# Local attention products with V: two heads in one matmul, or one head per matmul in four tiles

## The chip, the core and the metric

The kernel runs on one core of one Trainium2 chip. The metric is the device time of one execution in microseconds (us). PE is the matrix engine (TensorE), PEld its weight loads, DVE, ACT, POOL and SP are the vector, scalar, GpSimd and sync engines.

## What is computed

Attention over 8 batches, 8 heads, 576 positions and 64 values per head, in float32. In heads 0 to 3 a query sees itself and the 31 positions before it ("local"); in heads 4 to 7 it sees the earlier positions that are equal to its own modulo 32 ("strided"). The result, 4608 tokens of 512 values, goes through a mixture of 8 experts: every token takes the expert with the largest gate logit, its output is scaled by that gate probability.

```python
attn = softmax(where(mask, scale * q @ k.T, -1e9))      # mask local for h < 4, else strided
x = (attn @ v).transpose(0, 2, 1, 3).reshape(4608, 512)
expert_idx = argmax(x @ w_gate, axis=1)
for e in range(8):
    xe = x[expert_idx == e]
    out[expert_idx == e] = gate_w * (relu(xe @ w1[e]) @ w2[e])
```

## The kernel before, in words

**Attention (kind "A" in the planner).** Each batch has two local head pairs (`hp` 0 and 1), two strided ones, and five score banks of 128x512. A bank goes through: scores on PE (L713, L719 local, L728 strided), maximum and subtraction on DVE (L768, L773), exp on ACT (L777), sum and reciprocal on DVE (L781 to L784), normalization on POOL (L788), four transposes on PE (L793), and a copy to the tile `pT` (L295 or L297, in `evac`).

**Products with V.** `local(hp)` in `av_ops` multiplies the probabilities of 16 query blocks of 32 with V. Line 849 takes both heads of the pair in one matmul: the weights are 64 keys by 128 values (two heads of 64), the moving side 64 columns (two heads by 32 queries). Half of each 128x64 result is one head's V with the other head's probabilities and is never read. A float32 matmul shows in the trace as two passes, so a unit (one batch, one head pair) has 32 matmul records and 32 weight loads, and there are 16 units. Two tiles work side by side: `y` 0 on partitions 0 to 63, `y` 1 on 64 to 127. Four copies of 64x256 (`e_ev`, two `y` by two heads) bring the halves that count to `xT`. `strided(hp)` does the same with the helper `av_mm` (L816), which takes one head per matmul at tile position (64y, 64h), so four tiles; with `hp` 0 it also holds the last 64 local queries of both pairs, with 64 weight columns and 32 moving columns. Nothing of `strided` changes.

**Experts.** `window` handles 256 or 512 tokens of one expert, `slot` 128. A weight chunk of 1 MB (`raw`) is loaded by SP, rounded by ACT (`whi`, L384), its remainder taken by DVE (`wlo`, L388), and PE does three matmuls for every product (L507 to L509, L480 to L482; L579 to L581 and L607 to L609 in slots). Four windows (kind "F") are planned while attention still runs, once the tokens of the first four batches are routed; all other work (kind "B") after attention.

**The order of the work** is written out by a planner before the kernel is built. `add(engine, cost, emit, deps, get=, put=, prio=, ins=)` enters a piece of work with an estimated cost in ns; `Line.pick` takes the piece that can start first, by priority among those close together, and `issue` emits it. So each engine's order of instructions is fixed by these estimates; the chip keeps only the data dependences.

**Instructions.** `Line.fetch` models that PE's instructions come in blocks of 256 over DMA. `ins` counts a piece's PE instructions (a pass and its weight load are two). When a piece crosses into the next block, its cost grows by what is missing until `next_block`; then the next block is set to arrive 3500 ns later, plus the backlog that the planner sees on the DMA queues (`self.bus - began`), up to a cap. `PIECES` is 4, so the cap is 625 ns.

```python
if n and self.count >= 256:
    self.count -= 256
    at = t + cost * left / n
    still = max(0.0, self.next_block - at)
    began = at + still
    self.next_block = began + 3500.0 + min(max(0.0, self.bus - began), 2500.0 / PIECES)
```

Of the kernel before, what the change touches and what calls it, by code (L numbers as in the profile page):

```python
# [23 lines left out]
QB = 32  # L24
# [20 lines left out]
PIECES = 4  # L45
# [19 lines left out]
PE, ACT, DVE, POOL, SP = "PE", "ACT", "DVE", "POOL", "SP"  # L65
EITHER = (ACT, DVE)
# [21 lines left out]
class Line:  # L88
# [20 lines left out]
    def add(self, *a, **k):  # L109
        op = Op(*a, **k)  # L110
        self.pending[op.kind] += 1
        for d in op.deps:
            if d.done is None:
                op.left += 1
                d.users.append(op)
            else:
                op.ready = max(op.ready, d.done + self.LAG[d.where])
        if not op.left:
            self.waiting.append(op)
        return op  # L120
# [60 lines left out]
    def fetch(self, t, n, cost):  # L181

        still = 0.0
        left = 256 - self.count
        self.count += n
        if n and self.count >= 256:
            self.count -= 256
            at = t + cost * left / n
            still = max(0.0, self.next_block - at)
            began = at + still  # L190
            self.next_block = began + 3500.0 + min(max(0.0, self.bus - began), 2500.0 / PIECES)
        return still

    def issue(self, t, e, op):
# [41 lines left out]
def act_ns(n):  # L236
    return 25 + 0.91 * n


def dve_ns(n):  # L240
    return 68 + 1.04 * n


def both(n):
    return {ACT: act_ns(n), DVE: dve_ns(n)}
# [31 lines left out]
def moe_attn(ctx, tc, lqk, vl, sqk, vs, wg, wcat, blob, out):  # L277
    nc = tc.nc
# [8 lines left out]
    def bank(slot):  # L287
        return ps.tile([128, 512], F32, name=f"b{slot.which}", bufs=1)

    def buf(pool, shape, dt, name, slot):  # L290
        return pool.tile(shape, dt, name=f"{name}{slot.which}", bufs=1)

    def evac(e, out, in_):
        if e == DVE:
            nc.vector.tensor_copy(out=out, in_=in_)  # L295
        else:
            nc.scalar.copy(out=out, in_=in_)  # L297
# [36 lines left out]
    add = line.add  # L334
# [301 lines left out]
    U = {}  # L636
# [35 lines left out]
    loads = {}  # L672
# [138 lines left out]
    def probs_of(b, pair, y, cols):  # L811
        k, n = WHERE[pair]
        return U[b, "pT", k][64 * y:64 * y + 64, 128 * n + cols.start:128 * n + cols.stop]

    def av_mm(av, c0_, w, h, y, lhsT, rhs):
        nc.tensor.matmul(av[64 * h:64 * h + 64, c0_:c0_ + w], lhsT, rhs, start=True, stop=True, tile_position=(64 * y, 64 * h))  # L816

    xslots = {}
    evs = {}

    def x_tile(g):
        if g not in xslots:
            xslots[g] = Slot("xT", 0)
        return xslots[g]

    def av_ops(b):
        g, bb = divmod(b, GB)
        off = bb * S
        xs = x_tile(g)
        evs.setdefault(g, {})[bb] = []  # L830

        def xT():
            if ("xT", g) not in U:
                U["xT", g] = buf(xtp, [128, 4, GB * S], F32, "xT", xs)
            return U["xT", g]

        def local(hp):
            st = {}

            def e_av(_):  # L840
                xT()
                vt = U[b, "vl", hp]
                st["av"] = [bank(x) for x in vsl]
                for m in range(4):
                    for i in range(2):
                        n = 2 * m + i
                        for y in range(2):
                            both_heads = probs_of(b, ("l", hp, m), y, slice(0, 128)).rearrange("p (h i q) -> p h i q", h=2, i=2)
                            nc.tensor.matmul(st["av"][y][:, 64 * n:64 * n + 64], vt[64 * y:64 * y + 64, n, :],  # L849
                                             both_heads[:, :, i, :], start=True, stop=True, tile_position=(64 * y, 0))  # L850

            vsl = [Slot("b", 2), Slot("b", 2)]
            get = list(vsl)
            if bb == 0 and hp == 0:
                get.append(xs)
            p = time_of(b, hp + 0.2)
            a = add(PE, 960, e_av, [U[b, "C", hp], loads[b, "vl", hp][0]], get=get, ins=64,
                    put=[U[b, "ps", hp], loads[b, "vl", hp][1]], prio=p)
            for y in range(2):
                for h in range(2):  # L860
                    def e_ev(e, y=y, h=h):
                        hs = slice(64 * h, 64 * h + 64)
                        dst = xT()[hs, hp, off:off + 512].rearrange("p (n y q) -> p n y q", y=2, q=QB)[:, :, y, :]
                        evac(e, dst, st["av"][y][hs, :].rearrange("p (n h q) -> p n h q", h=2, q=QB)[:, :, h, :])

                    evs[g][bb].append(add(EITHER, both(256), e_ev, [a], put=[vsl[y]], prio=p + 1))

        def strided(hp):
            st = {}
            c1 = 5 * RG  # L870

            def e_av(_):
                vst = U[b, "vs"]
                av = st["av"] = [bank(x) for x in vsl]
                for t in range(5):
                    for y in range(2):
                        for h in range(2):
                            av_mm(av[y], RG * t, RG, h, y, vst[64 * y:64 * y + RG, 5 * hp + t, 64 * h:64 * h + 64],
                                  probs_of(b, ("s", hp, t), y, slice(64 * h, 64 * h + RG))[0:RG])
                if hp == 0:  # L880
                    for i in range(2):
                        vt = U[b, "vl", i]
                        for y in range(2):
                            for h in range(2):
                                av_mm(av[y], c1 + QB * i, QB, h, y, vt[64 * y:64 * y + 64, 8, 64 * h:64 * h + 64],
                                      probs_of(b, ("lx", 0, 4), y, slice(64 * h + 32 * i, 64 * h + 32 * i + 32)))
                else:
                    for y in range(2):
                        for h in range(2):
                            av_mm(av[y], c1, LASTG, h, y, vst[64 * y:64 * y + LASTG, 10, 64 * h:64 * h + 64],  # L890
                                  probs_of(b, ("sx", 0, 5), y, slice(64 * h, 64 * h + LASTG))[0:LASTG])

            vsl = [Slot("b", 2), Slot("b", 2)]
            p = time_of(b, 3.2 + hp)
            deps = [loads[b, "vs"][0]] + ([U[b, "C", 2], U[b, "C", 3], loads[b, "vl", 0][0], loads[b, "vl", 1][0]] if hp == 0
                                          else [U[b, "C", 3], U[b, "C", 4]])
            put = [loads[b, "vs"][1]] + ([U[b, "ps", 2], U[b, "ps", 3], loads[b, "vl", 0][1], loads[b, "vl", 1][1]] if hp == 0
                                         else [U[b, "ps", 3], U[b, "ps", 4]])
            a = add(PE, 950 if hp == 0 else 770, e_av, deps, get=vsl, put=put, prio=p, ins=112 if hp == 0 else 96)
            for y in range(2):  # L900
                def e_ev(e, y=y):
                    xv = xT()[:, 2 + hp, off:off + S].rearrange("p (a r) -> p r a", r=STR)
                    dst = xv[:, 0:30, :].rearrange("p (t y l) a -> p t y l a", y=2, l=3)[:, :, y, :, :]
                    evac(e, dst, st["av"][y][:, 0:c1].rearrange("p (t l a) -> p t l a", l=3, a=SR))

                def e_ev2(e, y=y):
                    av = st["av"][y]
                    if hp == 0:
                        x0 = off + 512 + QB * y
                        evac(e, xT()[:, 0:2, x0:x0 + QB], av[:, c1:c1 + 2 * QB].rearrange("p (a q) -> p a q", q=QB))  # L910
                    else:
                        xl = xT()[:, 2 + y, off:off + S].rearrange("p (a r) -> p r a", r=STR)
                        evac(e, xl[:, 30:32, :], av[:, c1:c1 + LASTG].rearrange("p (r a) -> p r a", a=SR))

                evs[g][bb].append(add(EITHER, {ACT: 440, DVE: 620}, e_ev, [a], put=[vsl[y]], prio=p + 1))
                evs[g][bb].append(add(EITHER, both(80), e_ev2, [a], put=[vsl[y]], prio=p + 1))

        local(0)
        local(1)
        strided(0)  # L920
        strided(1)
# [306 lines left out]
    with tc.manual_schedule():  # L1228
# [9 lines left out]
        for b in range(B):  # L1238
# [5 lines left out]
            g, bb = divmod(b, GB)  # L1244
            p, f = time_of(b + 1, 2), 2000.0
            if g == EG - 1:
                p, f = (time_of(b, NBK - 0.5), 100.0) if bb else (time_of(b + 1, 0), 2000.0)
# [32 lines left out]
        start = F_START + F_SPAN * len(EXP)  # L1280
# [185 lines left out]
```

## Time and profile before

| what | value |
|---|---|
| median of 3 runs | 696.97 us (695.48 to 701.06) |
| profiled execution | 694.56 us, its span 692.4 us |
| PE matmuls busy | 645.1 us (93%), 6468 records |
| DVE / ACT / POOL busy | 408.2 / 374.8 / 167.0 us |
| local products with V (L849) on PE | 512 records, 34.4 us |

The span runs from the first to the last instruction; the execution's own time is 2.2 us longer. The trace gives start and duration of every instruction, what ended an engine's idle time ("<-"), and the chain of work that ended last. "issue" in that chain is time in which the engine waited for nothing that the profile shows.

### The profile page before, as it was taken

The page shows a single profiled execution, that of the slowest core. Times are in us where ns is not written, and L with a number is a line of the kernel's source. Part 1 is how long each engine was busy: PE and PEld are TensorE (multiplying, and loading weights), DVE is VectorE, ACT ScalarE, POOL GpSimd, SP SyncE. Part 2 cuts the span into 40 slices and gives each one's busy share as a digit, 9 for nine tenths or more (in the row PEclk, how much of TensorE's full clock was granted, in tenths as well). Part 3 has the DMA queues.
Part 4 walks back from the last instruction along what each step waited for, and adds up shares of the span by engine and source line. Part 5 has one row for each costly group of instructions (what it writes and reads, how often), then busy time and mean ns, then how long its engine had stood idle before and what let it go on. Part 6 is the DMA issues. An engine that isn't in the chain of part 4 may idle for free.

```text
span 692.4 us, 15650 instructions
## 1 busy us (share of the span) xinstructions
PE 645.1 (93%) x6468; PEld 546.1 (79%) x6472; DVE 408.2 (59%) x752; ACT 374.8 (54%) x675; POOL 167.0 (24%) x232
## 2 busy tenths in 40 slices
PE   5899798999999997799999999998999999999993
PEld 4677677789888886698888888887888888978882
DVE  5577777684756669774327565246573347664271
ACT  2566466574746663654337474256582366663471
POOL 2222534530414226412015021042030051110120
PEclk9999999599999999999999999999999999999998
DMA  9968959972675455987246867337776258582430
GB/s 300 325 196 281 311 173 385 371 251 78 218 235 194 161 183 167 382 294 239 68 136 228 279 235 270 122 127 269 244 257 235 75 203 320 202 292 74 137 122 6
DMA packets 84170, 149.60 MB, mean 216 GB/s; under 512 B 4861, under 2 KB 33533, under 8 KB 84096
## 3 DMA queue, kind: packets, MB, share of 16 engines
q1 hardware_dynamic: 75264, 124.73, 53.6%
q0 software_dynamic: 6432, 20.26, 7.8%
q10 hardware_dynamic: 2400, 3.58, 1.5%
q8 instruction: 52, 0.85, 0.5%
q14 instruction: 22, 0.18, 0.1%
HBM read 129.38 MB, written 20.22 MB: 216 GB/s over the span
## 4 chain that ended last, share of the span: by engine, by line
PE 78%; DMA 6%; DVE 5%; issue 4%; ACT 3%; POOL 2%; another core or an unknown queue 0%; POOLq 0%; SPq 0%; ACTq 0%; DVEq 0%
PE b L482 8%; PE b L480 8%; PE b L509 8%; PE b L481 8%; PE b L507 8%; PE b L508 7%; PE b L849 5%; DMA raw<-in_wcat_dram 5%; PE b L728 3%; DVE wlo L388 3%; PE b L719 3%; PE b L793 2%; PE b L456 2%; PE b L993 2%; PE b L580 2%
## 5 line engine op out<-in xcount | busy, mean ns | idle before, releaser
L388 DVE TENSOR_TENSOR wlo<-raw,whi 128x1024 fp32r<-128x1024 f32 x160 | 190.9, 1226 | 84.3 <-ACT whi L384 81.3
L384 ACT CAST whi<-raw 128x1024 fp32r<-128x1024 f32 x160 | 163.5, 1053 | 63.9 <-PE b L482 46.4
L507 PE MATMUL b<-xh,whi 128*128 128x256 f32 (+1 forms) x384 | 125.5, 327 | 0.0
L509 PE MATMUL b<-xh,wlo 128*128 128x256 f32 (+1 forms) x384 | 123.3, 321 | 1.8 <-DVE wlo L388 1.5
L508 PE MATMUL b<-xl,whi 128*128 128x256 f32 (+1 forms) x384 | 122.5, 319 | 0.3 <-DVE xl L352 0.3
L480 PE MATMUL b<-whi,hh 128*128 128x512 f32 x256 | 103.1, 403 | 3.2 <-ACT hh L517 3.1
L482 PE MATMUL b<-whi,hl 128*128 128x512 f32 x256 | 101.3, 396 | 4.1 <-DVE hl L520 4.1
L517 ACT ACTIVATE hh<-b 128x256 fp32r<-128x256 f32 (+1 forms) x96 | 43.4, 453 | 107.8 <-PE b L509 103.1
L481 PE MATMUL b<-wlo,hh 128*128 128x512 f32 x256 | 100.2, 391 | 0.0
L520 DVE SCALAR_TENSOR_TENSOR hl<-b,hh 128x256 fp32r<-128x256 f32 (+1 forms) x96 | 48.2, 506 | 73.3 <-ACT hh L517 73.2
L423 POOL DMA_INDIRECT out_dram<-y,oids x24 | 24.9, 1039 | 240.9 <-ACT y L416 237.9
L509 PEld LDWEIGHTS b<-xh,wlo 128*128 128x128 f32 x384 | 72.9, 190 | 9.2 <-DVE wlo L388 3.7
L508 PEld LDWEIGHTS b<-xl,whi 128*128 128x128 f32 x384 | 73.0, 190 | 7.5 <-DVE xl L352 0.5
L507 PEld LDWEIGHTS b<-xh,whi 128*128 128x128 f32 x384 | 72.9, 190 | 6.9
L788 POOL TENSOR_TENSOR prob<-prob,ri 128x512 f32<-128x512 f32 x40 | 43.3, 1082 | 103.8 <-DVE ri L784 79.5
L482 PEld LDWEIGHTS b<-whi,hl 128*128 128x128 f32 x256 | 48.0, 188 | 17.4 <-DVE hl L520 6.3
L297 ACT COPY xT<-b 64x256 f32<-64x256 f32 (+3 forms) x122 | 42.8, 418 | 34.8 <-PE b L849 20.7
L480 PEld LDWEIGHTS b<-whi,hh 128*128 128x128 f32 x256 | 48.3, 189 | 11.9 <-ACT hh L517 4.3
L481 PEld LDWEIGHTS b<-wlo,hh 128*128 128x128 f32 x256 | 48.4, 189 | 8.1
L352 DVE TENSOR_TENSOR xl<-b,xh 128x256 fp32r<-128x256 f32 (+1 forms) x48 | 23.4, 505 | 30.3 <-ACT xh L350 27.4
L781 DVE TENSOR_REDUCE sm<-prob 128x8 f32<-128x512 f32 x40 | 27.0, 676 | 18.8 <-ACT prob L777 18.5
L579 PE MATMUL b<-whi,sxh 128*128 128x256 f32 x128 | 37.6, 294 | 0.0
(164 smaller groups left out, 1044.0 us busy)
## 6 DMA issues: line engine op xcount, KB each, us to landing
raw<-in_wcat_dram SPq DMA_DIRECT2D x80, 1024.0 KB, 8.5
lqk_sb<-in_lqk_dram SPq DMA_DIRECT2D x16, 592.0 KB, 5.8
sqk_sb<-in_sqk_dram SPq DMA_DIRECT2D x16, 576.0 KB
vt<-in_vl_dram SPq DMA_DIRECT2D x16, 576.0 KB, 5.1
xd<-xr SPq DMA_DIRECT2D x24, 264.0 KB, 5.6
vst<-in_vs_dram SPq DMA_DIRECT2D x8, 704.0 KB, 11.3
xd<-xr ACTq DMA_DIRECT2D x12, 264.0 KB, 2.0
xg<-xd,ids POOLq DMA_INDIRECT x24
```

What stands on the lines that cost most here:

```text
L297: nc.scalar.copy(out=out, in_=in_)
L384: nc.scalar.copy(out=self.hi[:, sl], in_=self.raw[:, sl])
L388: nc.vector.tensor_tensor(out=self.lo[:, sl], in0=self.raw[:, sl], in1=self.hi[:, sl].bitcast(F32), op=ALU.subtract)
L480: nc.tensor.matmul(Y[t], H["h"][:, ts], ch.hi[:, w], start=(j == 0), stop=False)
L481: nc.tensor.matmul(Y[t], H["h"][:, ts], ch.lo[:, w], start=False, stop=False)
L482: nc.tensor.matmul(Y[t], H["l"][:, ts], ch.hi[:, w], start=False, stop=(j == 7))
L507: nc.tensor.matmul(b, ch.hi[:, w], X["h"][:, dc, :], start=(dc == 0), stop=False)
L508: nc.tensor.matmul(b, ch.hi[:, w], X["l"][:, dc, :], start=False, stop=False)
L509: nc.tensor.matmul(b, ch.lo[:, w], X["h"][:, dc, :], start=False, stop=(dc == 3))
L517: nc.scalar.activation(out=H["h"][:, 0:n], in_=H["b"][:, 0:n], func=AF.Relu)
L520: nc.vector.scalar_tensor_tensor(out=H["l"][:, 0:n], in0=H["b"][:, 0:n], scalar=0.0, in1=H["h"][:, 0:n].bitcast(F32), op0=ALU.max, op1=ALU ...
L788: nc.gpsimd.tensor_tensor(out=pv, in0=pv, in1=st["ri"].unsqueeze(2).broadcast_to([128, 8, 64]), op=ALU.mult)
```

## The change

In `local`, line 849 becomes a loop over the two heads that calls `av_mm`: 64 weight columns, 32 moving columns, tile position (64y, 64h). Each unit then has 32 matmuls (64 passes and 64 weight loads) on four tiles in place of 16 on two. Both heads of a `y` land in the 128 partitions of one bank, so two copies of 128x256 take the place of four of 64x256. The planner's numbers follow: cost 960 becomes 1070, `ins` 64 becomes 128, and a bank is given back after one copy, not two. Apart from that, the cap in `fetch` goes from 625 to 2500 ns.

```diff
-            self.next_block = began + 3500.0 + min(max(0.0, self.bus - began), 2500.0 / PIECES)
+            self.next_block = began + 3500.0 + min(max(0.0, self.bus - began), 2500.0)
...
                         for y in range(2):
-                            both_heads = probs_of(b, ("l", hp, m), y, slice(0, 128)).rearrange("p (h i q) -> p h i q", h=2, i=2)
-                            nc.tensor.matmul(st["av"][y][:, 64 * n:64 * n + 64], vt[64 * y:64 * y + 64, n, :],
-                                             both_heads[:, :, i, :], start=True, stop=True, tile_position=(64 * y, 0))
-
-            vsl = [Slot("b", 2), Slot("b", 2)]
+                            for h in range(2):
+                                av_mm(st["av"][y], QB * n, QB, h, y, vt[64 * y:64 * y + 64, n, 64 * h:64 * h + 64],
+                                      probs_of(b, ("l", hp, m), y, slice(64 * h + 32 * i, 64 * h + 32 * i + 32)))
+
+            vsl = [Slot("b"), Slot("b")]
...
-            a = add(PE, 960, e_av, [U[b, "C", hp], loads[b, "vl", hp][0]], get=get, ins=64,
+            a = add(PE, 1070, e_av, [U[b, "C", hp], loads[b, "vl", hp][0]], get=get, ins=128,
                     put=[U[b, "ps", hp], loads[b, "vl", hp][1]], prio=p)
             for y in range(2):
-                for h in range(2):
-                    def e_ev(e, y=y, h=h):
-                        hs = slice(64 * h, 64 * h + 64)
-                        dst = xT()[hs, hp, off:off + 512].rearrange("p (n y q) -> p n y q", y=2, q=QB)[:, :, y, :]
-                        evac(e, dst, st["av"][y][hs, :].rearrange("p (n h q) -> p n h q", h=2, q=QB)[:, :, h, :])
-
-                    evs[g][bb].append(add(EITHER, both(256), e_ev, [a], put=[vsl[y]], prio=p + 1))
+                def e_ev(e, y=y):
+                    dst = xT()[:, hp, off:off + 512].rearrange("p (n y q) -> p n y q", y=2, q=QB)[:, :, y, :]
+                    evac(e, dst, st["av"][y][:, 0:256].rearrange("p (n q) -> p n q", q=QB))
+
+                evs[g][bb].append(add(EITHER, both(256), e_ev, [a], put=[vsl[y]], prio=p + 1))
```

## Rows read from the trace of the kernel before

**Rows 1.** Page: busy time and records of each engine, DMA in 40 slices, instruction queue.

```profile
PE 645.1 (93%) x6468; PEld 546.1 (79%) x6472; DVE 408.2 (59%) x752; ACT 374.8 (54%) x675; POOL 167.0 (24%) x232
...
DMA  9968959972675455987246867337776258582430
...
q8 instruction: 52, 0.85, 0.5%
```

**Rows 2.** Stretches: length, busy us (records) PE, PEld, DVE, ACT, POOL; clock, DMA share, GB/s.

```profile
10.00:30.00 20.00, 15.48 (x369) 12.94 (x362) 12.81 (x28) 9.84 (x23) 6.24 (x6) 0.91 1.03 341
...
50.00:62.00 12.00, 11.30 (x272) 9.21 (x272) 8.86 (x21) 7.90 (x21) 3.13 (x3) 1.00 0.89 292
...
100.00:140.00 40.00, 36.76 (x680) 30.19 (x680) 28.13 (x76) 25.55 (x58) 18.06 (x29) 0.79 1.06 376
...
160.00:260.00 100.00, 99.52 (x1072) 86.51 (x1074) 62.37 (x136) 61.66 (x119) 25.02 (x39) 1.00 0.53 184
260.00:300.00 40.00, 31.73 (x195) 27.20 (x194) 32.50 (x84) 19.47 (x32) 20.23 (x24) 0.96 0.82 285
```

**Rows 3.** Line 849 alone in such stretches: busy us (records) of PE and PEld.

```profile
10.00:30.00 20.00, 4.41 (x64) 4.09 (x64) 0.91 1.03 341
30.00:50.00 20.00, 4.00 (x64) 3.73 (x64) 0.91 0.77 239
50.00:62.00 12.00, 4.24 (x64) 3.96 (x64) 1.00 0.89 292
...
100.00:140.00 40.00, 9.25 (x124) 8.79 (x126) 0.79 1.06 376
...
160.00:230.00 70.00, 4.00 (x64) 3.73 (x64) 1.00 0.56 193
```

**Rows 4.** Chain that ended last, 91 to 126 us: start, us, what.

```profile
91.14 1.03 PE b L719 x64
...
94.66 0.44 issue
...
102.60 1.93 PE b L849 x32
...
116.06 1.80 issue
117.86 1.48 PE b L816 x79
...
119.66 1.56 PE b L728 x32
121.22 0.83 PE b L1089 x9
...
122.48 1.44 issue
123.92 1.74 PE b L728 x32
```

**Rows 5.** The same chain over the whole span.

```profile
28.28 1.87 issue
...
74.75 2.51 issue
...
128.14 3.61 PE b L849 x32
...
145.03 0.95 PE b L816 x56
...
274.41 16.20 DMA raw<-in_wcat_dram
```

**Rows 6.** PE's matmuls in order, 145.5 to 146 us.

```profile
145.59 0.40 PE L816 MATMUL b<-pT,vt 64*64 64x32 f32 x16
145.91 0.33 PE L456 MATMUL b<-cst,xg 128*128 128x128 f32 x1
```

**Rows 7.** Groups of instructions by line and shape: busy us, mean ns; idle before.

```profile
L297 ACT COPY xT<-b 64x256 f32<-64x256 f32 x63 | 23.1, 366 | 21.9 <-PE b L849 20.7 <-POOL key L1071 0.5
```

## The prediction

> **What bounds the kernel now.** I read the page's busy times first: PE 645.1 us of 692.4, DVE 408.2, ACT 374.8 [rows 1]. PE is the bound; the DMA slices are full only in parts of the first 140 us. The view by stretches then splits attention in two. From 160 to 260 us expert work is mixed in, and PE is busy 99.52 us of 100. Before that it idles: 4.5 us of 20 in 10 to 30, 3.2 of 40 in 100 to 140, where the granted clock is also 0.79 on the mean (part of it at 1.2 GHz, the rest at 2.4) [rows 2]. The chain shows what those gaps are: "issue" pieces of 1.87, 2.51, 0.44, 1.80 and 1.44 us, 8.06 us in all [rows 4, 5]. They are waits for instructions. Between the stalls that end at 117.86 and 123.92 the chain has 79, 32 and 9 matmul passes and two single ones, 122; with one weight load each 244 instructions, which with some semaphores is the planner's block of 256 [rows 4]. The whole kernel fits that: 6468 + 6472 records over 52 transfers of the instruction queue is 249 each [rows 1].
>
> So a block has a price of its own. With the DMA share at 1.06 [rows 2] one took 123.92 - 117.86 = 6.06 us to arrive. In the quieter place around 94.66, counting 122 passes back leads into the score group that began at 91.14, so that block took at most 94.66 + 0.44 - 91.14 = 3.96 us [rows 4]. A block that PE needs longer than that to work off costs nothing; a shorter one leaves a stall.
>
> **The matmuls.** A unit of line 849 takes 1.93 us undisturbed [rows 4], 60 ns per pass, and once 3.61 us at the low clock [rows 5]. The four-tile form is in the trace: the strided unit's 56 passes take 0.95 us, 17 ns each [rows 5]; 64 of those are 1.09 us. Its 16 passes with exactly the new shape (64 weight columns, 32 moving) run from 145.59 to 145.91, 20 ns each with the switch to the next work [rows 6]; 64 of those would be 1.28 us. The cheapest neighbour is the local score group, 64 passes in 1.03 us [rows 4]. I take 1.08, near the 56-pass row, since a long run dilutes the switch: 0.85 us less per unit, 13.6 us for 16 units (bounds 0.65 and 0.90: 10.4 and 14.4).
>
> Rows say that a pass with 32 moving columns on four tiles is 17 to 20 ns apart from the next. The Trainium skill, TensorEngine Tiling (Array Packing), section Instruction Overhead, says that every matmul carries about 60 cycles and that no factor should be taken from a dimension already small, which the 64 moving columns are. By it 64 passes would be 64 x 25 ns = 1.60 us at 2.4 GHz and the 16 units would save 5.3 us, an estimate from that page; the rows disagree and decide.
>
> **The instructions.** A unit goes from 64 to 128 instructions: 16 x 64 = 1024, four blocks more. Line 849 was cover: at 60 ns per pass 256 instructions last 7.7 us, above the 6.06 that a block takes under load. The new form would use up 256 in 4.3 us, below it. So each unit is worth something else by place [rows 3]:
> - Loaded stretches (10 to 30, 50 to 62, 100 to 140; DMA share 0.89 to 1.06): eight units, 2 + 2 + 4. They hold 369 + 272 + 680 matmul records [rows 2], twice that in instructions, 2642 or 10.3 blocks in 72 us: 7.0 us per block, little above 6.06. With 8 x 64 = 512 more there are 12.3 blocks, and 12.3 x 6.06 = 74.6 us. Even evenly spread, instructions alone would need 2.6 us more than the stretches take now. PE's own saving there, 8 x 0.85 plus some 0.9 for the unit at the low clock, 7.7 us, is the other bound. I take +2.6: the measured stalls show the limit is already touched, and the price of 6.06 is the one nearest to these stretches.
> - Quiet attention (30 to 50 and 80 to 90, two units each; DMA share 0.77 in the first): a block arrives in under 4 us, so 4 x 0.85 = 3.4 us are saved.
> - After 140 us, four units (two of them in 160 to 230), beside expert matmuls that fill PE and use few instructions: again 3.4 us.
>
> **The copies.** Half of the 64 go. ACT's 63 took 366 ns each [rows 7], so 32 x 0.366 = 11.7 us. ACT is half idle, so on the path this is nothing; but ACT stood 20.7 us waiting for line 849 [rows 7], in order, with exps and other copies behind it. The planner charged 960 ns for 1930, so it queued those copies too early; 1070 fits the new 1080. A unit that ends 0.85 us earlier frees ACT for the next bank's exp. I credit 1 us (0 to 3).
>
> **The cap of 2500.** It adds no instruction to the chip; it only changes the order. The planner's 3.5 to 6.0 us per block covers the 3.96 and 6.06 of the trace, where the old 4.125 did not. Nothing shows the new order. Bounds: all 8.06 us of instruction stalls gained, or another hole at the change from attention to experts, where PE idled 8.3 us of 40 [rows 2] behind a weight load of 16.20 us on the chain [rows 5]. I take 0 between ends of equal size.
>
> **Sum.** +2.6 - 3.4 - 3.4 - 1 = -5.2 us against the profiled 694.56 (its span 692.4): 689.4. The median of the runs shown is 2.4 us above the profiled time, so 691.8; I say 691.5. From there on PE is busy nearly throughout, so what attention gains reaches the end.
>
> **Rivals.**
> - *The matmul gain arrives whole.* Blocks keep ahead of PE, as they do in the quiet stretch: -13.6 - 0.9 - 1 = -15.5 us, or 681.5; half-hidden stalls give 684 to 687. For it: at 7.0 us per block some 20 blocks pass before 140 us, and only five stalled; and 72 us of loads are a fixed number of bytes, so a late block may fall into a quieter time. Against: the five stalls. This is the rule of the Trainium skill, Runtime: NRT & Kernel Launch, section Instruction fetch mechanics, that crossing a block's edge is mostly hidden; the stalls of 1.4 to 2.5 us contradict it under load and agree with it elsewhere. Chance 0.28.
> - *Instruction blocks set the pace of attention* (slower). It decides if blocks take 6.06 us wherever attention runs alone: 12 units there then cost 64/256 x 6.06 = 1.5 us each and save nothing, +18.2 - 3.4 = +14.8 us, or 712. With the eight loaded units alone it is +12.1 - 6.8 = +5.3, 702. For it: 7.0 against 6.06 us in the loaded stretches, and a low clock after the stalls at 116 and 122 us. Against: 3.96 us at 91. Its middle is 705; chance 0.17.
> - *The new order outweighs both edits' direct cost,* by up to 8 us either way around the sum: 683 or 700. Chance 0.10.
> - *Nothing to be saved in the matmul,* since four tiles run no faster at 32 columns: the 20 ns row still saves 10.4 us of PE, so this hardly changes the sign. It lies inside the range.
>
> **How the numbers follow.** The forecast, most of the gain eaten by instruction blocks (-2 to -9 us, 688 to 695), has 0.45. A change of 1% is 7 us, about what a measurement of this kernel can tell: below 690 is faster, above 704 slower. Faster: 0.28 from the first rival, 0.09 of the forecast, 0.04 of the new order, 0.41. Slower: 0.13 of the second rival and 0.03 of the order, 0.16. Same: 0.43. The range runs from the full gain with little spare, 680, to the second rival's middle, 704.
>
> **What the changed profile would show.** Line 816's helper takes the local units: 64 passes in about 1.08 us, PE's sum lower by 13 to 15 us. 56 instruction transfers in place of 52. More or longer "issue" pieces on the chain before 150 us: 8 us now, 15 to 20 if the forecast holds, unchanged if the first rival does. The first expert matmuls of line 507 come 2 to 5 us earlier. ACT's wait for the local unit falls well below 20.7 us. I am wrong if the loaded stretches keep blocks under 5 us, or if the gap at 260 to 300 us changes by more than the 8.3 it has.

## The result: 0.6% slower, and the profile after

The changed kernel takes 703.59 us (median of 20 runs, 695.97 to 710.03) against 698.32 us for the kernel before in the same comparison. The ratio of the two is 1.0063 [1.0040, 1.0086], with a 95% interval: 4.4 us slower. It leaves out the four slow executions of the changed kernel, and the profiled one (granted clock 0.956 on the mean, 0.973 in before's) is one of them. The time is inside the range forecast (680 to 704) and inside the 1% called no change, but the direction forecast, 5 us faster, is wrong, and the interval excludes any gain.

The two profiled executions, 694.56 and 706.74 us (span 705.0), lie 12.2 us apart; before's is 3.8 us below its median in this comparison and after's 3.2 above, so rows of the two must not be made to explain more than 4.4 us, and after's lower clock is not taken for a cause.

The page of the changed kernel: busy time and records of each engine, the granted clock in 40 slices, the instruction queue.

```profile
PE 642.6 (91%) x6981; PEld 539.1 (76%) x6984; DVE 412.9 (59%) x752; ACT 364.9 (52%) x643; POOL 167.6 (24%) x232
...
PEclk9897978679999999999999999999999999999998
...
q8 instruction: 56, 0.92, 0.5%
```

Against [rows 1] it has 513 more matmul records, 4 more instruction transfers and 32 fewer ACT operations, all as worked out beforehand. PE's sum is only 2.5 us lower, not 13 to 15.

The same stretches as [rows 2], of the changed kernel (length, busy us and records of PE, PEld, DVE, ACT, POOL, then clock, DMA share, GB/s), and ahead of them the first 160 us:

```profile
0.00:160.00 160.00, 127.93 (x3323) 102.09 (x3326) 105.62 (x259) 77.61 (x171) 53.58 (x77) 0.84 0.83 273
10.00:30.00 20.00, 13.26 (x392) 10.75 (x396) 12.26 (x29) 8.04 (x18) 5.56 (x6) 0.89 0.97 319
50.00:62.00 12.00, 9.40 (x215) 7.20 (x211) 6.83 (x15) 7.01 (x17) 3.85 (x4) 0.77 0.94 312
100.00:140.00 40.00, 31.52 (x741) 23.96 (x737) 34.19 (x79) 21.83 (x48) 21.07 (x27) 0.81 1.03 349
160.00:260.00 100.00, 98.32 (x1319) 83.72 (x1321) 62.98 (x130) 57.48 (x111) 24.90 (x36) 1.00 0.55 176
260.00:300.00 40.00, 32.60 (x224) 27.21 (x224) 32.52 (x104) 21.03 (x39) 20.92 (x28) 0.96 0.67 239
```

In the same three windows of time PE is less busy than in [rows 2] (13.26 for 15.48, 9.40 for 11.30, 31.52 for 36.76). Over 160 us PE has 11.87 us less work (before: 139.80, shown below). The twelve units done by then add 384 records and only 176 more are there: by that count, though the order is another, PE is behind in its program, not ahead. The chain shows what stands in the gaps. Its longer "issue" pieces and two lines beside them (start, us, what):

```profile
18.33 3.34 issue
...
26.69 1.36 issue
...
54.66 2.07 issue
...
90.13 0.99 issue
...
103.94 1.06 PE b L816 x64
...
108.27 1.74 issue
...
119.58 3.07 issue
...
128.78 0.59 issue
...
133.16 2.54 issue
...
138.25 0.54 issue
...
285.99 16.21 DMA raw<-in_wcat_dram
```

With two more of 0.53 us (at 42.23 and 50.13) they are eleven pieces over half a microsecond before 150 us, 17.30 us together, where the five of [rows 4] and [rows 5] were 8.06. The local unit's 64 passes take 1.06 us for 1.93 [rows 4]. The weight load at the change from attention to experts is as long as in [rows 5], but starts at 285.99 and not 274.41.

The copies, by line and shape (busy us, mean ns, idle before):

```profile
L297 ACT COPY xT<-b 128x256 f32<-128x256 f32 x32 | 10.5, 375 | 14.3 <-PE b L816 12.6 <-PE b L793 1.7
```

Half as many as in [rows 7], at the same price each, and ACT's wait for the local unit is 12.6 us where it was 20.7.

### The profile page after: what moved, and what is told of

Read it like the earlier page. It is cut to its first block, busy times and chain, and to the rows that moved or that the text cites. A ratio compares the mean times of both kernels' runs of the same rounds, so it can differ in the third digit from the quotient of the medians.

```text
span 705.0 us, 16639 instructions
## 1 busy us (share of the span) xinstructions
PE 642.6 (91%) x6981; PEld 539.1 (76%) x6984; DVE 412.9 (59%) x752; ACT 364.9 (52%) x643; POOL 167.6 (24%) x232
## 4 chain that ended last, share of the span: by engine, by line
PE 78%; issue 6%; DVE 6%; DMA 4%; ACT 3%; POOL 2%; another core or an unknown queue 0%; SPq 0%; POOLq 0%; ACTq 0%; DVEq 0%
PE b L480 8%; PE b L509 8%; PE b L482 8%; PE b L507 8%; PE b L481 8%; PE b L508 8%; PE b L816 5%; DMA raw<-in_wcat_dram 3%; PE b L793 3%; PE b L719 3%; PE b L728 2%; DVE wlo L388 2%; PE b L991 2%; PE b L456 2%; PE b L580 2%
## 5 line engine op out<-in xcount | busy, mean ns | idle before, releaser
L508 PEld LDWEIGHTS b<-xl,whi 128*128 128x128 f32 x384 | 73.1, 190 | 10.3 <-DVE ri L784 3.0
L788 POOL TENSOR_TENSOR prob<-prob,ri 128x512 f32<-128x512 f32 x40 | 41.8, 1047 | 108.5 <-DVE ri L784 68.8
L777 ACT ACTIVATE prob<-prob 128x512 f32<-128x512 f32 x40 | 25.2, 634 | 37.7 <-DVE prob L773 37.5
L297 ACT COPY xT<-b 128x256 f32<-128x256 f32 (+3 forms) x89 | 29.5, 439 | 25.5 <-PE b L816 23.7
L768 DVE TENSOR_REDUCE nm<-b 128x8 f32<-128x512 f32 x40 | 26.9, 677 | 22.6 <-PE b L719 15.6
```

What stands on the lines that cost most here:

```text
L508: nc.tensor.matmul(b, ch.hi[:, w], X["l"][:, dc, :], start=False, stop=False)
L788: nc.gpsimd.tensor_tensor(out=pv, in0=pv, in1=st["ri"].unsqueeze(2).broadcast_to([128, 8, 64]), op=ALU.mult)
```

## The experiments

The change has three parts that were parted: the four-tile matmuls, the new costs and slots given to the planner (with the merged copies), and the longer modelled delay (2500 for 625 ns, the "cap" of the expectations). The delay, the costs and the slots act on the chip only through the order of the work; the merged copies also take 32 copies away. The theories were: instruction blocks eat the matmul gain (A), later in the form that the place of a unit, loaded or quiet, decides; the new order costs (B); the place does not matter (C); the cost of order grows with the modelled delay (D) or any redrawn order is worse by chance (E); a block of instructions waits behind load packets (F) or for bandwidth (G); the low clock costs. All ratios below are to the kernel before in the same comparison, on the same chip, with 95% intervals. The expectations name some runs by number: e12 is the quiet and late units with delay 0, e13 all units a second time, e14 the quiet and late units a second time, e16 the delay of 2500 a second time.

**The matmuls alone, in the order of before.** The planner's numbers and the four copies to a unit stay.

```
-  both_heads = probs_of(...).rearrange("p (h i q) -> p h i q", h=2, i=2)
-  nc.tensor.matmul(st["av"][y][:, 64 * n:64 * n + 64], vt[64 * y:64 * y + 64, n, :], both_heads[:, :, i, :], ...)
+  for h in range(2):
+      av_mm(st["av"][y], QB * n, QB, h, y, vt[64 * y:64 * y + 64, n, 64 * h:64 * h + 64], probs_of(...))
-  evac(e, dst, st["av"][y][hs, :].rearrange("p (n h q) -> p n h q", h=2, q=QB)[:, :, h, :])
+  evac(e, dst, st["av"][y][hs, 0:256].rearrange("p (n q) -> p n q", q=QB))
```

> Four-tile matmuls in the order of the kernel before: only the emitted matmuls and the columns that the four copies read change; the planner is told the old cost, ins and cap, so every engine's order is that of before. Theory A (instruction blocks take back what the matmuls save, and more, while loads run): time within -3 to +6 us of before (695 to 704), instruction stalls on PE before 160 us 14 to 22 us against 8. Theory B (the new order is what costs; the matmuls by themselves gain): 6 to 14 us faster than before (684 to 692), stalls below 11 us.

Measured 697.21 us, 1.0000 [0.9966, 1.0033], as theory A expected. PE's sum is 10.3 us lower than in [rows 1], and none of that arrives. The page of this kernel, and its stretches:

```profile
PE 634.8 (91%) x6980; PEld 535.7 (77%) x6984; DVE 409.8 (59%) x752; ACT 375.2 (54%) x675; POOL 166.8 (24%) x232
```

```profile
0.00:160.00 160.00, 125.84 (x3502) 101.35 (x3506) 108.21 (x271) 88.83 (x204) 55.46 (x80) 0.93 0.84 278
30.00:50.00 20.00, 15.47 (x463) 12.08 (x452) 11.06 (x28) 9.94 (x25) 4.07 (x7) 0.91 0.80 256
80.00:90.00 10.00, 8.61 (x234) 6.72 (x228) 9.05 (x24) 6.51 (x16) 5.30 (x7) 1.00 1.01 332
140.00:160.00 20.00, 17.29 (x486) 13.85 (x485) 14.36 (x33) 12.83 (x32) 6.34 (x7) 0.89 0.79 263
```

The kernel before, where it was not shown yet:

```profile
0.00:160.00 160.00, 139.80 (x3147) 114.67 (x3151) 110.14 (x283) 91.52 (x213) 55.89 (x83) 0.91 0.85 281
30.00:50.00 20.00, 19.00 (x424) 15.02 (x424) 12.81 (x30) 10.65 (x25) 4.64 (x7) 0.91 0.77 239
80.00:90.00 10.00, 10.00 (x138) 8.56 (x138) 6.42 (x20) 5.57 (x14) 3.53 (x6) 0.90 0.66 228
140.00:160.00 20.00, 20.00 (x452) 16.34 (x451) 15.54 (x41) 14.09 (x37) 7.63 (x9) 1.00 0.59 194
```

In 160 us PE has 13.96 us less work (139.80 - 125.84). It has 355 more records; before has fourteen units behind it by then, so the same place in the program would be 448 more, and PE has got no further. (This execution took 700.78 us and before's 694.56, though the medians agree: the rows show where PE waits, not the total.) The three stretches at 30, 80 and 140 us had 1.0 us of idle PE before and have 8.63 now. PE's waits for instructions in the first 160 us (us, times, longest), first the kernel before, then this one:

```profile
PE b L816 <- issue: 6.6, 4, 2.5
...
PE b L728 <- issue: 1.7, 2, 1.4
...
PE b L719 <- issue: 0.5, 1, 0.5
```

```profile
PE b L719 <- issue: 11.1, 9, 2.7
PE b L816 <- issue: 10.5, 9, 2.6
...
PE b L728 <- issue: 0.5, 2, 0.3
```

8.8 us have become 22.1: 13.3 us more of waiting against 13.96 us less of work. Its chain has thirteen "issue" pieces over half a microsecond before 160 us, 19.18 us together; those that fall into these stretches or on their edge are:

```profile
30.67 1.19 issue
...
35.97 2.64 issue
...
87.37 1.12 issue
...
143.58 2.71 issue
```

That these are waits for instruction blocks can be counted in the trace. Of the thirteen, all but one (1.14 us at 135.39) end 190 to 192 records past a multiple of 256, with weight loads and semaphore waits counted among PE's records. The stalls that end at 31.86 and 38.61 us are one block apart, so that block took 6.75 us, in a stretch that the forecast called quiet.

The mean clock over these 160 us is 0.93, no lower than before's 0.91. So the low clock of the changed kernel's profile (0.84) isn't needed to lose the matmul gain.

**After's order with the old matmuls**, the copies two to a piece; and **the change without the longer delay**:

```
  # first kernel, from after: the matmul of before at line 849, and in e_ev
+  for h in range(2):
+      hs = slice(64 * h, 64 * h + 64)
+      dst = xT()[hs, hp, off:off + 512]...
+      evac(e, dst, st["av"][y][hs, :].rearrange("p (n h q) -> p n h q", h=2, q=QB)[:, :, h, :])
  # second kernel, from after
-  self.next_block = began + 3500.0 + min(max(0.0, self.bus - began), 2500.0)
+  self.next_block = began + 3500.0 + min(max(0.0, self.bus - began), 2500.0 / PIECES)
```

> The order of the changed kernel with the two-head matmuls and their four copies (two to a piece). Theory A: the order is worth little, within 3 us of before (695 to 701), stalls near 8 us. Theory B: the order costs by itself, 5 to 15 us slower than before (703 to 713), and slower than the changed kernel, since the matmuls' 13.6 us come on top.

> The changed kernel with the planner's cap back at 625 ns. Theory A: as the changed kernel, within 3 us (700 to 706), since no instruction goes away. Theory B, in the form that the cap made the order bad: 5 us or more faster than the changed kernel.

The first measured 712.47 us, 1.0207 [1.0154, 1.0260]; the second 701.83 us, 1.0060 [1.0030, 1.0090]. The new order by itself costs 2.1%. That is not instruction stalls, of which this kernel has 7.8 us in the first 160 us:

```profile
PE b L719 <- issue: 4.4, 3, 2.7
...
PE b L728 <- issue: 1.9, 2, 1.5
...
PE b L849 <- issue: 1.5, 1, 1.5
```

Its largest wait there is for the normalization on POOL (line 788), 7.8 us for 3.9 in the kernel before. In that order the four-tile matmuls and the merged copies together do earn something, 712.47 to after's 703.59 across two comparisons, 1.4% by the two ratios; in the order of before the matmuls earn nothing. The parts don't add up, and no one of them can be given "its" share: it depends on the path. By the path matmuls (0.0 us), then copies, costs and slots (+4.2, the second kernel here), then the longer delay (+0.2, the change), the 4.4 us are all in the middle step. That step has 27.5 us of PE's waits for instructions in the first 160 us, 5.4 more than the matmuls alone. Merged copies in the order of before were not run, so copies, costs and slots stay one step. With the new costs, the longer delay changes nothing that can be measured (1.0060 and 1.0063).

**The longer delay alone, and other delays.** In the kernel before, `2500.0 / PIECES` (625) becomes 2500.0, 1250.0 or 0.0; the first and the last were run twice.

> The kernel before with the cap at 2500 ns. Theory A: within 3 us of before (695 to 701), stalls near 8 us. Theory B, in the form that the cap made the order bad: 4 us or more slower than before.

> The kernel before with the cap at 0 ns, so that the planner counts on a block every 3.5 us; the order changes in about as many places as with 2500. Theory D (a longer delay in the plan makes the order worse, step by step): the same as before or faster, 690 to 699. Theory E (the order of before is a good draw and any redrawn order is worse): 4 to 12 us slower, 701 to 709.

> The kernel before with the cap at 1250 ns. Theory D: between before and the cap of 2500 (1.2% slower), 699 to 705. Theory E: anywhere from 697 to 710, with no step between 625 and 2500.

> Cap 0 in the kernel before. Theory D (a longer modelled delay makes the order worse): 0.2 to 0.6% faster than before, 1.4 to 2% faster than e16. Theory E (a redrawn order is worse by chance): anywhere, here 0 to 1% slower.

> Cap 2500 in the kernel before. Both theories: 0.8 to 1.6% slower than before, as in e4.

Measured: 2500 gives 1.0120 [1.0080, 1.0159] (707.42 us) and 1.0103 [1.0069, 1.0136] (692.19); 1250 gives 1.0071 [1.0030, 1.0112] (691.04); 0 gives 0.9962 [0.9935, 0.9989] (685.81) and 0.9974 [0.9936, 1.0012] (685.79). With the costs of before, the more delay the planner reckons with, the slower the kernel, although nothing of the delay is executed. That is as D expected (delay 0 the second time is level within its interval). Every setting is another order, so four in a row can still be chance, and with the new costs the same delay changed nothing. What goes with it is where the expert products stand. Line 507 alone (PE and PEld only) from 200 to 250 us, then all engines there; first the kernel before, then 2500, then 0:

```profile
200.00:250.00 50.00, 13.46 (x45) 8.36 (x45) 1.00 0.48 171
200.00:250.00 50.00, 49.83 (x619) 42.87 (x620) 29.97 (x56) 31.29 (x59) 10.50 (x13) 1.00 0.48 171
```

```profile
200.00:250.00 50.00, 9.85 (x32) 6.35 (x32) 0.97 0.48 163
200.00:250.00 50.00, 45.90 (x646) 38.19 (x646) 29.46 (x57) 26.82 (x56) 14.63 (x20) 0.97 0.48 163
```

```profile
200.00:250.00 50.00, 16.16 (x57) 10.62 (x57) 1.00 0.48 165
200.00:250.00 50.00, 48.66 (x459) 43.36 (x460) 27.96 (x50) 27.46 (x51) 7.11 (x11) 1.00 0.48 165
```

With 2500 the planner uses expert products earlier, as filler for stalls that it now believes in. By 200 us the two runs of 2500 have 228 and 246 records of expert matmuls, the kernel before 220, the two runs of 0 157 and 168; of all other matmuls they have 3147 and 3149, 3297, and 3510 twice. So less of attention is done by then, and fewer expert products are left beside the last attention banks (32 records, 45, 57). PE is then idle 4.1 us of the 50, where it was 0.17. The last matmul group of the routing, line 1089, first the kernel before, then 2500 and 2500 a second time (last start at the end of the line's times):

```profile
L1089 PEld LDWEIGHTS <-am x36: 95/98/145, 81.8 to 266.0; 128*128 128x128 bf16 x36
```

```profile
L1089 PEld LDWEIGHTS <-am x36: 95/98/99, 82.9 to 277.4; 128*128 128x128 bf16 x36
```

```profile
L1089 PEld LDWEIGHTS <-am x36: 95/102/145, 80.2 to 269.6; 128*128 128x128 bf16 x36
```

In the first run routing ends 11 us later, and the experts behind it with it; in the second only 3.6 us later than in before's trace, with a ratio almost as large. So the late routing is not shown to be the cause: it is one execution's size, and with delay 0 PE is idle 1.34 us there and the kernel is no slower. No experiment kept the delay and moved the expert products back.

**Which units gain.** The four-tile form in some batches only, order of before: `if b in (1, 3, 6, 7):` (the quiet stretches and what comes after 140 us), `if b >= 6:`, `if b in (0, 2, 4, 5):` (the loaded stretches), with the two-head form in the `else`. All sixteen units and the first of these were repeated.

> The order of before; the four-tile matmuls only in batches 1, 3, 6 and 7, the eight units that the prediction put in quiet stretches or after 140 us. Theory A, by place (a unit saves 0.85 us where blocks arrive in time, and only the loaded ones give it back): 4 to 7 us faster than before. Theory C (a block more costs the same wherever it comes, since a late block in one place only moves the stall on): within 2 us of before, like the swap of all 16.

> The order of before; the four-tile matmuls only in batches 6 and 7, the four units from 149 us on, beside expert matmuls. Theory A: 3.4 us faster (2 to 5). Theory C: no change (within 2 us).

> The order of before; the four-tile matmuls only in batches 0, 2, 4 and 5, the eight units under loads. The swap of all 16 gave no change, and the other eight alone 0.9% faster. Theory A, by place: 3 to 8 us slower than before (0.4 to 1.2%). Theory C (half of the units, wherever they are, is cheaper than all): 2 to 6 us faster.

> Four-tile matmuls in all 16 units in the order of before, a second time. Theory A and C both: within 0.4% of before. If the chip decides: like e14.

> Four-tile matmuls in batches 1, 3, 6 and 7, a second time. Theory A (the place of a unit decides): 0.6 to 1.2% faster than before and faster than e13 by as much. If the gain was the chip's: within 0.3% of e13.

> Four-tile matmuls in batches 1, 3, 6 and 7, a third time. Theory A (the place of a unit decides): 0.3 to 1.0% faster than before. If it was the chip of the first two calls: within 0.3% of before.

Measured: quiet and late units 0.9913 [0.9872, 0.9954], 0.9956 [0.9912, 1.0000] and 0.9991 [0.9949, 1.0033]; late ones alone 0.9963 [0.9933, 0.9993]; loaded ones 0.9992 [0.9958, 1.0026]; all again 1.0016 [0.9984, 1.0048]. The gains of 0.4 to 0.9% came only in comparisons where the kernel before took 687 to 688 us (684.35, 685.56 and 684.67 us); by the medians of all runs the two of the quiet and late units are 0.6 and 0.2%. In the third, where it took 696.11, the same file showed none (696.32). Loaded units, run where before took 698.25 us, cost nothing, against the 2.6 us forecast for them and against both expectations (A slower, C faster). In the comparison that had both, all units were level and the quiet and late ones 0.4% faster: there the place may decide, as A has it. That quiet units gain is not established.

**Smaller packets.** `PIECES = 8` for 4, the delay held at 625, without and with the four-tile matmuls; it tests whether a block of instructions waits behind the packet of a load.

> The kernel before with every load cut in 8 pieces, not 4 (packets half as long; the planner's cap held at 625 ns, so the order is that of before). Theory F (a block of instructions waits behind the data packets of its DMA engine): blocks under load arrive in 4 to 5 us, stalls below 5 us, time 0 to 6 us better unless the shorter packets slow the loads. Theory G (the wait is for bandwidth, not for packets): stalls as before, 7 to 9 us, time the same or worse.

> Four-tile matmuls in all 16 units in the order of before, loads in 8 pieces. Theory F: the stalls that took the gain back shrink to under 10 us, and it is 5 to 12 us faster than the same matmuls with 4 pieces, so 5 to 12 us faster than before. Theory G: within 3 us of before with 8 pieces, stalls 14 us or more.

Measured 1.0070 [1.0035, 1.0106] (702.24 us) and 1.0123 [1.0093, 1.0153] (706.30). PE's waits for instructions in the first 160 us (us, times, longest), of the one and of the other:

```profile
PE b L816 <- issue: 7.4, 5, 2.7
...
PE b L728 <- issue: 2.5, 2, 2.3
```

```profile
PE b L719 <- issue: 16.1, 9, 3.3
PE b L816 <- issue: 7.7, 5, 2.7
```

With 0.5 us more at line 728 of the other, 9.9 and 24.3 us, longest 2.7 and 3.3, where the same two with four pieces have 8.8 and 22.1, longest 2.5 and 2.7: halved packets did not shorten a wait, so theory F fell, and they cost time of their own. What makes a block late stays open.

**The two best parts together**: four tiles in batches 1, 3, 6 and 7 with delay 0.

> Four-tile matmuls in batches 1, 3, 6 and 7 and the cap at 0. If the two gains add up: 1.2% faster than before (0.9 to 1.6%). If the new order moves the loads onto those batches: 0.4%, as the cap alone.

> The same with cap 0, so another order. If e12's loss came from the two parts together: 0.7 to 1.5% slower than before again. If the chip decided there: 0.5 to 1.3% faster, the sum of the two gains.

Measured 1.0106 [1.0074, 1.0139] (705.17 us) and 1.0218 [1.0152, 1.0283] (709.14). Two edits that were each level or a little faster are together 1 to 2% slower; the first time both theories had expected a gain. Both runs were made where before took 696 to 698 us, and delay 0 alone only where it took 687 to 688, so whether the pair or the setting is to blame stays open. No version beat the kernel before reliably.

## Why the prediction was wrong, point by point

- **The price of 64 passes** was right: 1.06 us for 1.08, 17 ns a pass. The Trainium skill, TensorEngine Tiling (Array Packing), section Instruction Overhead, gives every matmul about 60 cycles, which by an estimate from that page is 25 ns a pass at 2.4 GHz and 1.60 us a unit; the trace disagrees. In the matmuls alone the local products took 12.5 us less of PE (34.4 and 3.4 us before, 25.3 then).
- **Four more instruction blocks, and stalls of 15 to 20 us** were right: 56 transfers, 17.30 us. So was the price of a block under load, 6.06 us: from the end of one stall to the next, where one block lies between, the changed kernel has 6.38 (21.67 to 28.05), 6.72 (122.65 to 129.37) and 6.33 us (129.37 to 135.70). And so was the rule that a unit which uses its block up faster than the next arrives gains nothing. The Trainium skill, Runtime: NRT & Kernel Launch, section Instruction fetch mechanics, calls the crossing of a block's edge mostly hidden; the 22.1 us of waits in the matmuls alone disagree.
- **The terms for quiet attention and for the time after 140 us, -3.4 us each, failed** where the change was measured. The prediction let blocks arrive in under 4 us there, and wrote that the new form uses up 256 instructions in 4.3 us. But two units are 256 instructions and take 2 x 1.08 = 2.2 us, less than even a quiet block's 3.96; 4.3 counts passes without their weight loads. And the blocks were slower: 6.75 us for one in 30 to 50 us of the matmuls alone, where stalls of 1.19 and 2.64 us came, with 1.12 in 80 to 90 and 2.71 in 140 to 160. The DMA share of a stretch was taken as a given, but it rose from 0.66 to 1.01 in 80 to 90 and from 0.59 to 0.79 in 140 to 160; that the faster matmuls moved the loads there is the likely reading, not a shown one. The eight units measured -0.6 us, give or take 2.9, against -6.8 (0.9991, before at 696.11). Where before took 687 to 688 us they gave -6.0 and -3.0, and the late ones -2.5, so there the terms are not refuted.
- **The loaded term, +2.6,** measured about 0 (0.9992). The matmuls in all came to 0.0 us, give or take 2.3, for the -4.2 that these three terms add up to.
- **The new costs and slots** were costed at -1 us through the copies, and this term failed by sign. ACT's wait fell as forecast (12.6 for 20.7), but the new numbers redraw the order, and without the longer delay the change is 0.6% slower, +4.2 us, all of it on top of matmuls that earn nothing.
- **The cap of 2500, "I take 0",** came true by luck: on top of the new costs it added 0.2 us, but alone it costs 1.2 and 1.0%, by these ratios 8.4 and 7.1 us, the size of the bound of +8.3. I named that bound by the hole at 260 to 300 us, and the hole's own size hardly changed (7.4 us idle after, 8.3 before); it came later. Taking the middle of two equal ends was not a reading of the rows: PE was busy 99.52 us of 100 from 160 to 260 [rows 2], so a new order had little to gain there and much cover to lose.
- **The rivals.** The new order outweighing the rest (0.10, 700 us against a median of 697, so 3 us slower) came nearest to what happened: 4.4 us slower, from the order or the copies that go with it. The second rival's 702 for the loaded units alone is as near by number, but its cause is not: those units cost nothing.
- **Signposts.** First expert matmuls of line 507 come 2 to 5 us earlier: no, at 152.1 us for 151.6. PE's sum 13 to 15 lower: 10.3 in the matmuls alone, 2.5 after, where the mean clock over 160 us is 0.84 for 0.91. The blocks did not come faster under load and the hole did not change by 8.3, the two signs named for being wrong; neither was the one that mattered.

Shown by runs: the swap is worth nothing in the order of before, and its saving comes back as waits at the edges of instruction blocks; the change's new order costs by itself; with the costs of before the four delays tried are slower the longer they are. Argued only: that the early use of expert products is how. Open: which of costs, slots and merged copies makes the 4.2 us, why the swap with the merged copies earns 1.4% in the order of after, and whether quiet units gain.

## What to carry to other kernels

When you split matmuls into more tiles, count PE's instructions too: where PE already waits for instruction blocks, a slower matmul is cover for the next block, and the time saved comes back as waits, also in places that had none. A planner's cost is part of the kernel: test a new estimate in an unchanged order, and the new order with the unchanged work, before you credit either. Don't take the middle of wide bounds for a new order, least of all where the bounding engine is already full: of the orders tried here one (delay 0) was 0.3 to 0.4% faster and all others 0.6 to 2.1% slower.

## What the runs showed of the hardware beyond the forecast

Of the kernel before there are two speeds, 687 to 688 us in two comparisons and 696 to 698 in the others, and one chip showed both. They go with the number of semaphore updates in the traces: 6,450 to 6,488 in the eight kernels of the former, 5,786 to 5,942 in all others, before and after among them. The same file, quiet and late units, profiled at 699.02 us and at 682.38 us, shows what it does. Of the execution of 699.02 us, PE's wait, and ACT's operation in its timeline (start, us, what, idle before and releaser):

```profile
PE b L607 <- ACT shh L350: 7.1, 6, 1.5
```

```profile
371.13 0.37 ACT L350 CAST xh<-b 128x256 fp32r<-128x256 f32 x1 [1.91 <-PE b L593]
```

and of that of 682.38 us, which has no such wait of line 607:

```profile
361.19 0.37 ACT L350 CAST xh<-b 128x256 fp32r<-128x256 f32 x1 [1.02 <-PE b L456]
```

The operation needs line 456; with fewer updates a later matmul, of line 593, is what the profile shows as releasing it, and PE then waits for ACT behind it. None of the eight traces with more updates has this wait of line 607; all twelve others have it, 2.9 us (before) to 7.2 (the matmuls alone). So it can be part of the some 9 us between the speeds. Why the updates differ is not known here. It is why ratios are taken to the kernel before in the same comparison, and it may be why the gain of the quiet units came and went.
